# One TensorE-bound kernel: tanh rows by transposes in a second chunk, merged taps, a reordered tail, and a table of priority shifts

## The chip, the cores and the metric

The kernel runs on one core of one Trainium2 chip. TensorE (PE) multiplies matrices into PSUM; VectorE (DVE) and ScalarE (ACT) evict PSUM and do the elementwise work; GpSimd (POOL) does small copies and memsets; SyncE (SP) issues nearly all DMAs. The engines run beside each other, each through its own list in order, and wait for one another by semaphores. The metric is the device time of one execution in microseconds; the median of three runs is given, and one execution is profiled.

## The reference

The forward pass of a speech joint network and its gradients, all in bf16 with batch 2, 16000 time steps, width 256, 8 label positions:

```
h  = gelu(conv3(x, w1))[:, ::2]          # 3 taps, every second step kept
f  = gelu(conv3(h, w2))[:, ::2]          # 4000 steps remain
fe = f @ w_f ;  ge = g @ w_g
j  = tanh(fe[:, :, None, :] + ge[:, None, :, :])
out = j @ w_o                            # [2, 4000, 8, 256]
```

Returned are `out` and the gradients of x, w1, w2, g, w_f, w_g and w_o for a given `grad_out` of the shape of `out`.

## The kernel before

**Chunks.** The 2 × 4000 output steps are cut into 17 chunks (k = 0 to 16): one of 256 steps, fifteen of 512, one of 64. Chunk k goes through three stages. `stage_a` does both convolutions with gelu and its derivative, fe, and row-major copies for the weight gradients (FR, FER by transposes on TensorE, HRo and HRe by DMA transposes). `stage_j` does the joint network for four pairs of label positions: the tanh tile JT (feature-major, ACT, L643), its row-major twin JR, the product with w_o (OUT_SB), grad_out times w_o transposed (from GOT, a DMA transpose of GO), the tanh derivative 1 − JT² (JSQ, then NGZ and the sum ZS on DVE, ending as NGFE), and w_o's gradient GWO from JR and GO. `stage_de` does the backward pass: GF, GHe, GHo, the weight gradients (helper `wgrad`, sums ACC1, ACC2, ACCF by `acc_add`), and grad x (GX_SB). While chunk k is in `stage_j`, chunk k + 1 is in `stage_a` and chunk k − 1 in `stage_de`.

**JR in two ways.** For chunks in `TRANS` (only chunk 0 before) JR is made from JT by transposes on TensorE into a bf16 PSUM tile (psb) and a copy by ACT or DVE. For the others DVE adds FER and GEB (L667) and ACT takes a second tanh (L672); for these, `stage_a` also makes FER by eight transposes and one copy.

**The order of the work** is written by a planner, the class `Flow`. Each operation is recorded with its engine or engines, a cost in ns, what it reads and writes, the buffers it takes, and a priority: a due time in units of output steps (512 to a full chunk) set by `F.now` or `at`, plus a shift looked up in `SHIFT` by the stage's name and a part of it. `issue` is a list scheduler: with the costs it keeps a clock for each engine, and again and again takes the operation that can start first, by priority among equals. An operation with two engines (`evac`, and the square JSQ) goes to whichever can start it first. The result is one fixed list for each engine. Before the change `SHIFT` is empty.

The stages' names in that table: "a", "j" and "d" for `stage_a` of the next chunk, `stage_j`, and `stage_de` of the chunk before, followed by the step's number 0 to 3, "s" for the steps from 4 on, and "e" for the last ones; loads carry the step alone. Parts are "jt", "jr", "jsq", "gwo", "out" in `stage_j`, "late" for the gelu derivative, "dma", "xc", "go", "got" for transfers.

**Grad x.** For each block of rows and each pair of its four output offsets, twelve products of 256 columns by blocks of w1 transposed are formed, six to a PSUM tile; offset pairs read GHo and GHe.

**The end.** The last chunk's weight gradients are subtracted into staging tiles on DVE (L763) and stored by SP.

Of the kernel before, what the change touches and what calls it, by code (L numbers as in the profile page):

```python
# [30 lines left out]

class Op:
    __slots__ = ("eng", "cost", "fn", "deps", "soft", "succ", "left", "prio", "new", "bufs", "done", "work", "n",
                 "ready", "kind", "span")


class Flow:
# [27 lines left out]
        b.seq, s[0] = s[0], s[0] + 1  # L65
        return b

    def op(self, eng, cost, fn, r=(), w=(), new=(), at=None, work=0.0, after=(), kind=None, behind=(), sub=None):
        o = Op()
        o.eng = (eng,) if isinstance(eng, str) else tuple(eng)  # L70
        o.cost = cost if isinstance(cost, tuple) else (cost,) * len(o.eng)
        o.fn, o.new, o.work, o.n = fn, list(new), work, len(self.ops)
        o.prio = ((self.now if at is None else at) + self.shift.get((self.stage, sub), 0.0), o.n)
        o.succ, o.done, o.ready, o.kind, o.span = [], None, 0.0, kind, None
        deps, bufs = set(after), []
        for lst, wr in ((r, False), (w, True)):
            for x in lst:
                b, key = x if isinstance(x, tuple) else (x, None)
                for d, k, dw in b.log:
                    if (wr or dw) and (k is None or key is None or k == key):  # L80
                        deps.add(d)
                if b not in bufs:
                    bufs.append(b)
        for lst, wr in ((r, False), (w, True)):
            for x in lst:
                b, key = x if isinstance(x, tuple) else (x, None)
                if wr:
                    b.log = [e for e in b.log if not (key is None or e[1] == key)]
                b.log.append((o, key, wr))
        for b in o.new:  # L90
            b.born = o
        deps.discard(o)
        o.soft = ({b.born for b in bufs if b.born is not None} | set(behind)) - deps - {o}
        deps |= o.soft
        for b in o.new:
            if b not in bufs:
                bufs.append(b)
        o.deps, o.bufs = deps, bufs
        for b in bufs:
            b.users += 1  # L100
        o.left = len(deps)
        for d in deps:
            d.succ.append(o)
        self.ops.append(o)
        return o

    def issue(self):
# [10 lines left out]
        head = {c: 0 for c in queue}  # L118

        def put(o):  # L120
            o.ready = max((d.span[0] if d in o.soft else d.done for d in o.deps), default=0.0)
            for e in o.eng:
                avail[e].append(o)

# [83 lines left out]
def c_pe(ns):  # L208
    return sum(max(n / 2.4 + 2.5, 25.0) for n in ns)
# [11 lines left out]
def kernel(  # L221
# [28 lines left out]
    KT = 2  # L250
# [9 lines left out]
    sizes.append(NP - sum(sizes))  # L260
    assert sum(sizes) == NP

    SHIFT = {}
    TRANS = (0,)

    class Chunk:
        pass
# [70 lines left out]
    def fl(ap, A):  # L338
        return ap.rearrange("p (a c) -> p a c", a=A)
# [138 lines left out]
            r=rd, w=[(X, "m")], bytes_=(c.Pw - lo) * nr * 512, new=new, at=at, after=after)  # L478
        return X

    def rows(k, cls, name, SRC, lo, n, r, at=None, pe=0):
        R = buf(cls, [P, n if cls != "hro" else NB + 1, D], BF16, name)
        if pe:
            tr = psum(BF16)

            def trs(e):
                for a in range(n):
                    for kt in range(KT):
                        nc.tensor.transpose(out=tr[:pe, a * D + kt * P:a * D + (kt + 1) * P], in_=SRC[:, lo + a, kt, :pe],  # L489
                                            identity=ident[:])  # L490
            op("PE", c_pe([P] * (n * KT)), trs, r=(r or [SRC]) + [ident], w=[tr], new=[tr], at=at)
            evac(lambda: R[:pe, 0:n].rearrange("p a d -> p (a d)"), lambda: tr[:pe, 0:n * D], n * D, r=[tr], w=[R], new=[R], f=0.58)
            return R
        dma("SP", lambda: R[:, 0:n].rearrange("p a (k d) -> p (a k) d", d=P),
            lambda: SRC[:, lo:lo + n].rearrange("p a k c -> p (a k c)"), r=[SRC] if r is None else r, w=[R],
            bytes_=n * 65536, new=[R], transpose=True, at=at)
        return R

    def conv_gelu(c, taps, rd, h_buf, h_lo, g_buf, g_lo, news):
# [3 lines left out]
        for mt in range(KT):  # L503
            ps = psum()

            def mms(e, mt=mt, ps=ps):
                for k, (wt, rhs) in enumerate(taps):
                    mm(fl(ps[:, :W], A), wt(mt), rhs(), k == 0, k == len(taps) - 1)
            op("PE", c_pe([W] * len(taps)), mms, r=rd, w=[ps], new=[ps] + ([sq, s] + news if mt == 0 else []))
            op("ACT", c_act(W, True), lambda e, mt=mt, ps=ps: nc.scalar.activation(  # L510
                out=sq[:, 0:A, mt, :Pw], in_=fl(ps[:, :W], A), func=ACT.Square, scale=GELU_SQRT_K), r=[ps], w=[(sq, mt)])
            op("ACT", c_act(W, True), lambda e, mt=mt, ps=ps: nc.scalar.activation(  # L512
                out=h_buf[:, h_lo:h_lo + A, mt, :Pw], in_=fl(ps[:, :W], A), func=ACT.Gelu_apprx_tanh),
               r=[ps], w=[(h_buf, mt)])
            op("DVE", c_dve(W), lambda e, mt=mt, ps=ps: nc.vector.scalar_tensor_tensor(  # L515
                out=s[:, 0:A, mt, :Pw], in0=sq[:, 0:A, mt, :Pw], scalar=1.0, in1=fl(ps[:, :W], A),
                op0=ALU.add, op1=ALU.mult), r=[(sq, mt), ps], w=[(s, mt)])
# [19 lines left out]
    def stage_a(k, t0, dt):  # L537
# [51 lines left out]
            op("PE", c_pe([W] * KT), mms, r=[(FT, 0), (FT, 1), WF], w=[ps], new=[ps] + ([FE] if mt == 0 else []))  # L589
            evac(lambda mt=mt: FE[:, 0:A, mt, :Pw], lambda ps=ps: fl(ps[:, :W], A), W, r=[ps], w=[(FE, mt)])  # L590
        if k not in TRANS:
            S["FER"] = rows(k, "fer", "FER", FE, 0, A, [(FE, 0), (FE, 1)], pe=Pw)
        F.now = t0 + 0.5 * dt
        S["HRo"] = rows(k, "hro", "HRo", HTo, 0, A + 1, None)
        S["HRe"] = rows(k, "hre", "HRe", HTe, 0, A, None)
# [161 lines left out]
    def acc_add(ACC, key, acc_ap, ps, k, out):  # L757
        if k == NG - 1:
            t_ = buf({id(ACCF): "jr", id(ACC2): "jt", id(ACC1): "go"}[id(ACC)], [P, 2 * D], BF16, "stage")

            def flat():
                return t_[:]
            op("DVE", c_dve(512), lambda e: nc.vector.scalar_tensor_tensor(  # L763
                out=flat(), in0=acc_ap().rearrange("p k d -> p (k d)"), scalar=-1.0, in1=ps[:],
                op0=ALU.mult, op1=ALU.subtract), r=[(ACC, key), ps], w=[t_], new=[t_])
            dma("SP", lambda: out.rearrange("(dt p) n -> p dt n", p=P),
                lambda: flat().rearrange("p (k d) -> p k d", d=D), r=[t_], w=[], bytes_=131072)
        elif k == 0:
            evac(lambda: acc_ap().rearrange("p k d -> p (k d)"), lambda: ps[:], 512, r=[ps], w=[(ACC, key)])
        else:  # L770
            op("DVE", c_dve(512), lambda e: nc.vector.tensor_tensor(  # L771
                out=acc_ap().rearrange("p k d -> p (k d)"), in0=acc_ap().rearrange("p k d -> p (k d)"), in1=ps[:],
                op=ALU.add), r=[(ACC, key), ps], w=[(ACC, key)])

    def stage_de(k, t0, dt):
# [112 lines left out]
        if c.px is not None:  # L888
# [3 lines left out]
            op("POOL", 100.0, lambda e: nc.gpsimd.memset(GHz[:, :, c.px:c.px + 1], 0.0), w=[GHz])  # L892
            dma("SP", lambda: GHzR[:].rearrange("p (k d) -> p k d", d=P), lambda: GHz[:].rearrange("p k c -> p (k c)"),
                r=[GHz], w=[GHzR], bytes_=65536, transpose=True)
        rows4 = [[(GHo, 0, 0), (GHe, 0, 2)], [(GHo, 0, 1)], [(GHe, 1, 0), (GHo, 0, 2)], [(GHe, 1, 1)]]
        GX = None
        for bl, m in c.sblk:
            if bl % 2 == 0:
                GX = buf("gx", [P, 2, 4, D], BF16, "GX_SB")
            for cp in range(2):  # L900
                ps = psum()
                jobs = []
                for cj in range(2):
                    l = [(SRC, off, i, kt) for SRC, off, i in rows4[2 * cp + cj] for kt in range(KT)]
                    jobs += [(cj, n == 0, n == len(l) - 1) + a for n, a in enumerate(l)]

                def mms(e, jobs=jobs, ps=ps, bl=bl, m=m):
                    for cj, s_, e_, SRC, off, i, kt in jobs:
                        src = SRC[:, off + bl, kt, :m]
                        if GHz is not None and bl == 0 and off == 1 and i == 0:  # L910
                            src = GHz[:, kt, :m]
                        mm(ps[:m, cj * D:(cj + 1) * D], src, W1T[:, kt, i * D:(i + 1) * D], s_, e_)
                op("PE", c_pe([D] * len(jobs)), mms, r=[GHo, GHe, W1T] + ([GHz] if GHz is not None else []), w=[ps],
                   new=[ps] + ([GX] if cp == 0 and bl % 2 == 0 else []))
                evac(lambda m=m, cp=cp, GX=GX, bl=bl: GX[:m, bl % 2, 2 * cp:2 * cp + 2].rearrange("p c d -> p (c d)"),
                     lambda m=m, ps=ps: ps[:m, :], 512, r=[ps], w=[(GX, (bl % 2, cp))], scale=-1.0)
# [1 line left out]
            if bl % 2 == 1 or bl == A - 1:  # L918
# [13 lines left out]
                    put(0, Pw, 0, n)  # L932
                if c.ext and h == 0:
                    put(Pw, Pw + 1, 0, 3)
        for i in range(KK):
            def xl(da):
                return lambda a, m, d2: X[:m, 4 * a + da, d2 * P:(d2 + 1) * P]

            def he(a, m, i=i):
                return GHzR[:m, :] if GHzR is not None and i == 0 and a == 0 else GHeR[:m, a, :]  # L940
            wgrad(ACC1, i, lambda i=i: ACC1[:, i],
                  [(xl(i), rr(GHoR), c.sblk, [X, GHoR]),
                   (xl(i + 2), he, c.sblk, [X, GHeR] + ([GHzR] if GHzR is not None else []))], out_2[i])
            tick()

    def store(dst, src, r, scale=None):
        t_ = buf("gsq", [P, NB, KT, P], BF16, "g_sq")
# [180 lines left out]
```

## Time and profile before

| what | value |
|---|---|
| median of 3 runs | 798.06 us (797.32 to 798.76) |
| profiled execution | 797.41 us, its span 795.6 us |
| granted TensorE clock, mean | 0.996 |
| PE / weight loads busy | 774.8 / 559.2 us |
| DVE / ACT busy | 725.2 / 720.7 us |
| POOL busy | 67.5 us |

The span is from the first to the last instruction of the profiled execution. A PE matmul's end is modelled, so PE's busy time says when it had work, and its pace is read from the starts. Groups of instructions are named by line, engine, operation and tiles; nearly all matmuls stand under one helper's line (L336) and all copies out of PSUM under L345 or L347 (ACT) and L350 or L352 (DVE), so the tile's name tells them apart.

### The profile page before, as it was taken

The page shows a single profiled execution, that of the slowest core. Times are in us where ns is not written, and L with a number is a line of the kernel's source. Part 1 is how long each engine was busy: PE and PEld are TensorE (multiplying, and loading weights), DVE is VectorE, ACT ScalarE, POOL GpSimd, SP SyncE. Part 2 cuts the span into 40 slices and gives each one's busy share as a digit, 9 for nine tenths or more (in the row PEclk, how much of TensorE's full clock was granted, in tenths as well). Part 3 has the DMA queues.
Part 4 walks back from the last instruction along what each step waited for, and adds up shares of the span by engine and source line. Part 5 has one row for each costly group of instructions (what it writes and reads, how often), then busy time and mean ns, then how long its engine had stood idle before and what let it go on. Part 6 is the DMA issues. An engine that isn't in the chain of part 4 may idle for free.

```text
span 795.6 us, 16104 instructions
## 1 busy us (share of the span) xinstructions
PE 774.8 (97%) x5916; PEld 559.2 (70%) x5916; DVE 725.2 (91%) x1535; ACT 720.7 (91%) x1164; POOL 67.5 (8%) x227
## 2 busy tenths in 40 slices
PE   7989899999999999999999999999999999999996
PEld 6657578676776767768576685767868677687875
DVE  5899999998989989899998998989989999999964
ACT  6999999999898998989989899898999989899742
POOL 2020100101000010210100001010010100102010
PEclk9999999999999999999999999999999999999999
DMA  9999999999999999999999999999999999899994
GB/s 195 213 193 206 249 233 230 259 220 221 218 248 234 231 220 205 238 248 214 230 250 239 202 225 219 242 251 229 216 235 254 235 212 212 211 261 202 261 205 123
DMA packets 381811, 178.85 MB, mean 225 GB/s; under 512 B 307586, under 2 KB 375460, under 8 KB 379812
## 3 DMA queue, kind: packets, MB, share of 16 engines
q1 hardware_dynamic: 380788, 177.16, 99.7%
q8 instruction: 46, 0.75, 0.4%
q10 hardware_dynamic: 784, 0.39, 0.2%
q14 instruction: 33, 0.27, 0.1%
q0 software_dynamic: 160, 0.27, 0.1%
HBM read 51.42 MB, written 50.34 MB: 128 GB/s over the span
## 4 chain that ended last, share of the span: by engine, by line
PE 55%; ACT 24%; DVE 14%; issue 4%; DMA 3%; SPq 0%; DVEq 0%; ACTq 0%
PE ps L336 45%; PE GWO L336 8%; ACT JT L643 5%; ACT JR L672 4%; ACT JSQ L702 4%; ACT OUT_SB L345 3%; DVE g_s L515 3%; DVE NGZ L715 2%; ACT GX_SB L347 2%; ACT g_sq L510 1%; DVE ZS L732 1%; DMA GO<-in_grad_out_dram 1%; PE psb L489 1%; DMA out_dram<-OUT_SB 1%; DVE ACC L771 1%
## 5 line engine op out<-in xcount | busy, mean ns | idle before, releaser
L643 ACT ACTIVATE JT<-FE,GE 128x512 bf16<-128x512 bf16 (+4 forms) x288 | 190.7, 723 | 0.3 <-PE ps L336 0.3
L715 DVE SCALAR_TENSOR_TENSOR NGZ<-JSQ,ps 128x512 f32<-128x512 bf16 (+3 forms) x252 | 152.3, 613 | 1.6 <-PE ps L336 1.5
L336 PE MATMUL ps<-WO,JT 128*128 128x256 bf16 (+1 forms) x1008 | 150.0, 274 | 0.7 <-ACT JT L643 0.6
L336 PE MATMUL ps<-GOT,WOT 128*128 128x512 bf16 (+2 forms) x544 | 149.3, 363 | 0.4 <-DMA GOT<-GO 0.4
L672 ACT ACTIVATE JR<-JR 128x1024 bf16<-128x1024 bf16 (+1 forms) x124 | 136.2, 1101 | 12.8 <-DVE JR L667 12.8
L345 ACT CAST OUT_SB<-ps 128x512 bf16<-128x512 f32 (+1 forms) x215 | 132.7, 629 | 12.7 <-PE ps L336 12.5
L336 PEld LDWEIGHTS <-JT 128*128 128x128 bf16 (+1 forms) x1008 | 98.8, 98 | 57.9 <-issue 1.3
L702 ACT ACTIVATE JSQ<-JT 128x1024 bf16<-128x1024 bf16 (+2 forms) x123 | 128.7, 1046 | 10.0 <-DVE NGZ L715 7.7
L336 PE MATMUL GWO<-GO,JR 128*128 128x256 bf16 (+1 forms) x1008 | 131.4, 274 | 4.5 <-ACT JR L672 4.3
L732 DVE TENSOR_TENSOR ZS<-ZS,NGZ 128x1024 f32<-128x1024 f32 (+2 forms) x102 | 115.8, 1135 | 0.5
L336 PEld LDWEIGHTS <-JR 128*128 128x128 bf16 (+1 forms) x1008 | 98.0, 98 | 24.1 <-ACT JR L672 6.3
L336 PEld LDWEIGHTS <-W 128*128 128x128 bf16 x612 | 57.9, 98 | 59.7 <-issue 2.8
L515 DVE SCALAR_TENSOR_TENSOR g_s<-g_sq,ps 128x512 bf16<-128x512 bf16 (+2 forms) x102 | 65.1, 641 | 34.0 <-ACT HTo L512 32.7
L667 DVE TENSOR_TENSOR JR<-FER,GEB 128x1024 bf16<-128x1024 bf16 (+1 forms) x124 | 84.1, 684 | 3.1 <-PE GWO L336 2.3
L336 PE MATMUL ps<-XC,W 128*128 128x512 bf16 (+2 forms) x408 | 84.5, 362 | 1.7 <-DMA XC<-in_x_dram 1.7
L336 PEld LDWEIGHTS <-X 128*128 128x128 bf16 (+1 forms) x756 | 73.9, 98 | 9.0 <-DMA HRo<-HTo 0.2
L771 DVE TENSOR_TENSOR ACC<-ACC,ps 128x512 f32<-128x512 f32 x90 | 60.8, 684 | 20.1 <-PE ps L336 19.3
L336 PE MATMUL ps<-W1T,GHo 128*128 128x256 bf16 (+1 forms) x378 | 72.1, 273 | 0.0
L336 PE MATMUL ps<-W1T,GHe 128*128 128x256 bf16 (+1 forms) x376 | 71.8, 273 | 0.0
L510 ACT ACTIVATE g_sq<-ps 128x512 bf16<-128x512 f32 (+2 forms) x102 | 62.2, 610 | 8.6 <-PE ps L336 6.0
L336 PEld LDWEIGHTS <-WOT 128*128 128x128 bf16 x544 | 51.8, 98 | 22.9 <-DMA GOT<-GO 0.7
L347 ACT ACTIVATE GX_SB<-ps 128x512 bf16<-128x512 f32 (+1 forms) x98 | 59.2, 640 | 5.4 <-PE ps L336 4.9
(139 smaller groups left out, 1123.4 us busy)
## 6 DMA issues: line engine op xcount, KB each, us to landing
GO<-in_grad_out_dram SPq DMA_DIRECT2D x60, 512.0 KB, 5.6
out_dram<-OUT_SB SPq DMA_DIRECT2D x60, 512.0 KB, 6.1
X<-in_x_dram SPq DMA_DIRECT2D x15, 1088.0 KB, 7.4
out_dram<-GX_SB SPq DMA_DIRECT2D x30, 512.0 KB, 4.5
GO<-in_grad_out_dram SPq DMA_DIRECT2D x5, 256.0 KB, 5.3
GOT<-GO SPq DMA_TRANSPOSE x65, 4.7
out_dram<-OUT_SB SPq DMA_DIRECT2D x4, 256.0 KB, 3.5
XC<-in_x_dram SPq DMA_TRANSPOSE x62, 4.4
```

The costliest lines, as they stand in the source:

```text
L336: nc.tensor.matmul(ps_ap, lhsT=lhsT, rhs=rhs, start=start, stop=stop)
L345: nc.scalar.copy(out=dst(), in_=src())
L347: nc.scalar.activation(out=dst(), in_=src(), func=ACT.Copy, scale=scale)
L510: op("ACT", c_act(W, True), lambda e, mt=mt, ps=ps: nc.scalar.activation(out=sq[:, 0:A, mt, :Pw], in_=fl(ps[:, :W], A), func=ACT.Square, s ...
L515: op("DVE", c_dve(W), lambda e, mt=mt, ps=ps: nc.vector.scalar_tensor_tensor(out=s[:, 0:A, mt, :Pw], in0=sq[:, 0:A, mt, :Pw], scalar=1.0, ...
L643: nc.scalar.activation(out=fl(JT[:, j, mt, :W], A)[:, :, lo:hi], in_=FE[:, 0:A, mt, lo:hi], func=ACT.Tanh, bias=GE[:, b, mt, 2 * up + j:2 ...
L667: op("DVE", c_dve(n * 2 * D, 0.5), lambda e, lo=lo, n=n, m=m, JR=JR: nc.vector.tensor_tensor(out=JR[:m, 0:n], in0=S["FER"][:m, lo:lo + n]. ...
L672: op("ACT", c_act(n * 2 * D), lambda e, n=n, m=m, JR=JR: nc.scalar.activation(out=JR[:m, 0:n], in_=JR[:m, 0:n], func=ACT.Tanh), r=[JR], w= ...
L702: nc.scalar.activation(out=JSQ[:, :, :W], in_=JT[:, j, :, :W], func=ACT.Square)
L715: nc.vector.scalar_tensor_tensor(out=fl(zap(), A)[:, :, lo:hi], in0=fl(JSQ[:, d2, :W], A)[:, :, lo:hi], scalar=1.0, in1=fl(ps[:, :W], A)[: ...
L732: nc.vector.tensor_tensor(out=a, in0=a, in1=b, op=ALU.add)
L771: op("DVE", c_dve(512), lambda e: nc.vector.tensor_tensor(out=acc_ap().rearrange("p k d -> p (k d)"), in0=acc_ap().rearrange("p k d -> p ( ...
```

## The change

Six things, of which the last reaches everywhere:

- `TRANS` becomes `(0, 1)`: chunk 1 too gets JR by transposes and copies, and no FER.
- The planner takes a `lag`: FER's transposes count as ready 500 ns after fe's eviction, but for the first chunk.
- In the first chunk the square (g_sq) is due 8 units later than before, so that it goes behind gelu.
- In grad x the products that share a left operand and use adjacent blocks of w1 transposed are merged: two matmuls of 512 columns and two of 256 take the place of six of 256. The block at the border between the two batch entries, which has its own copy GHz, keeps one of its pairs apart.
- For the last chunk, two of the three w1 gradients are recorded ahead of grad x, and the last of them is stored by ACT's queue.
- `SHIFT` gets a table of priority shifts by stage and part.

In the built programs the total of PE's matmuls falls by 194: 252 fewer in grad x, 64 more transposes of JT, 8 fewer of FE, and two of the border block kept apart. The engine of 45 OUT_SB copies and 15 GX_SB copies changes from ACT to DVE. The other engines' counts follow from JR's way in chunk 1.

```diff
-    SHIFT = {}
-    TRANS = (0,)
+    SHIFT = {
+        ("1", "xc"): 32, ("2", "go"): -64, ("2", "got"): -272, ("a0", "late"): 256, ("a2", "dma"): 8,
+        ("a3", "late"): -32, ("ae", None): 64, ("ae", "late"): 64, ("as", "dma"): 320, ("as", "late"): 256,
+        ("d0", None): 32, ("d2", None): 16, ("j0", "jsq"): -32, ("j0", "out"): 8, ("j1", "jr"): 128,
+        ("j1", "jsq"): -256, ("j1", "out"): 64, ("j2", None): 48, ("j2", "dma"): 64, ("j2", "gwo"): -256,
+        ("j3", None): 128, ("j3", "dma"): -64, ("j3", "out"): -256, ("je", None): -32, ("je", "jt"): 8,
+        ("je", "out"): 64, ("js", None): -32, ("js", "gwo"): -248, ("js", "out"): 16, ("s", "go"): -16,
+        ("s", "got"): 64,
+    }
+    TRANS = (0, 1)
...
-            o.ready = max((d.span[0] if d in o.soft else d.done for d in o.deps), default=0.0)
+            o.ready = max((d.span[0] if d in o.soft else d.done for d in o.deps), default=0.0) + o.lag
...
-                out=sq[:, 0:A, mt, :Pw], in_=fl(ps[:, :W], A), func=ACT.Square, scale=GELU_SQRT_K), r=[ps], w=[(sq, mt)])
+                out=sq[:, 0:A, mt, :Pw], in_=fl(ps[:, :W], A), func=ACT.Square, scale=GELU_SQRT_K), r=[ps], w=[(sq, mt)],
+               at=F.now + 8.0 if c.first else None)
...
-            S["FER"] = rows(k, "fer", "FER", FE, 0, A, [(FE, 0), (FE, 1)], pe=Pw)
+            S["FER"] = rows(k, "fer", "FER", FE, 0, A, [(FE, 0), (FE, 1)], pe=Pw, lag=0.0 if c.first else 500.0)
...
-            dma("SP", lambda: out.rearrange("(dt p) n -> p dt n", p=P),
+            dma("ACT" if ACC is ACC1 and key == KK - 1 else "SP", lambda: out.rearrange("(dt p) n -> p dt n", p=P),
...
+        for i in range(2 if c.last else 0):
+            grad_w1(i)
...
-                def mms(e, jobs=jobs, ps=ps, bl=bl, m=m):
-                    for cj, s_, e_, SRC, off, i, kt in jobs:
-                        src = SRC[:, off + bl, kt, :m]
-                        if GHz is not None and bl == 0 and off == 1 and i == 0:
-                            src = GHz[:, kt, :m]
-                        mm(ps[:m, cj * D:(cj + 1) * D], src, W1T[:, kt, i * D:(i + 1) * D], s_, e_)
+                def mms(e, ps=ps, bl=bl, m=m, cp=cp, SA=SA, oa=oa, SB=SB, ob=ob):
+                    z = GHz is not None and bl == 0 and cp == 1
+                    for kt in range(KT):
+                        if z:
+                            mm(ps[:m, 0:D], GHz[:, kt, :m], W1T[:, kt, 0:D], kt == 0, False)
+                            mm(ps[:m, D:2 * D], SA[:, oa + bl, kt, :m], W1T[:, kt, D:2 * D], False, False)
+                        else:
+                            mm(ps[:m, 0:2 * D], SA[:, oa + bl, kt, :m], W1T[:, kt, 0:2 * D], kt == 0, False)
+                    for kt in range(KT):
+                        mm(ps[:m, 0:D], SB[:, ob + bl, kt, :m], W1T[:, kt, 2 * D:3 * D], False, kt == KT - 1)
...
-        for i in range(KK):
+        for i in range(2 if c.last else 0, KK):
+            grad_w1(i)
```

`grad_w1(i)` holds what the body of the old last loop held: one call of `wgrad` for tap i and one step of the due time.

More of the change, by code (lines that the diff above doesn't have):

```diff
@@ L33 @@
     __slots__ = ("eng", "cost", "fn", "deps", "soft", "succ", "left", "prio", "new", "bufs", "done", "work", "n",
-                 "ready", "kind", "span")
+                 "ready", "kind", "span", "lag")
 class Flow:
@@ L66, in buf, with op @@
         return b
-    def op(self, eng, cost, fn, r=(), w=(), new=(), at=None, work=0.0, after=(), kind=None, behind=(), sub=None):
+    def op(self, eng, cost, fn, r=(), w=(), new=(), at=None, work=0.0, after=(), kind=None, behind=(), sub=None, lag=0.0):
         o = Op()
@@ L73, in op @@
         o.prio = ((self.now if at is None else at) + self.shift.get((self.stage, sub), 0.0), o.n)
-        o.succ, o.done, o.ready, o.kind, o.span = [], None, 0.0, kind, None
+        o.succ, o.done, o.ready, o.kind, o.span, o.lag = [], None, 0.0, kind, None, lag
         deps, bufs = set(after), []
@@ L479, in load_x, with rows @@
         return X
-    def rows(k, cls, name, SRC, lo, n, r, at=None, pe=0):
+    def rows(k, cls, name, SRC, lo, n, r, at=None, pe=0, lag=0.0):
         R = buf(cls, [P, n if cls != "hro" else NB + 1, D], BF16, name)
@@ L490, in trs @@
                                             identity=ident[:])
-            op("PE", c_pe([P] * (n * KT)), trs, r=(r or [SRC]) + [ident], w=[tr], new=[tr], at=at)
+            op("PE", c_pe([P] * (n * KT)), trs, r=(r or [SRC]) + [ident], w=[tr], new=[tr], at=at, lag=lag)
             evac(lambda: R[:pe, 0:n].rearrange("p a d -> p (a d)"), lambda: tr[:pe, 0:n * D], n * D, r=[tr], w=[R], new=[R], f=0.58)
@@ L894, in stage_de, with grad_w1, xl, he @@
                 r=[GHz], w=[GHzR], bytes_=65536, transpose=True)
-        rows4 = [[(GHo, 0, 0), (GHe, 0, 2)], [(GHo, 0, 1)], [(GHe, 1, 0), (GHo, 0, 2)], [(GHe, 1, 1)]]
+        pairs4 = [(GHo, 0, GHe, 0), (GHe, 1, GHo, 0)]
+        def grad_w1(i):
+            def xl(da):
+                return lambda a, m, d2: X[:m, 4 * a + da, d2 * P:(d2 + 1) * P]
+            def he(a, m, i=i):
+                return GHzR[:m, :] if GHzR is not None and i == 0 and a == 0 else GHeR[:m, a, :]
+            wgrad(ACC1, i, lambda i=i: ACC1[:, i],
+                  [(xl(i), rr(GHoR), c.sblk, [X, GHoR]),
+                   (xl(i + 2), he, c.sblk, [X, GHeR] + ([GHzR] if GHzR is not None else []))], out_2[i])
+            tick()
+        for i in range(2 if c.last else 0):
+            grad_w1(i)
         GX = None
@@ L901, in stage_de @@
                 ps = psum()
[L902 to L905, printed above, removed]
-                def mms(e, jobs=jobs, ps=ps, bl=bl, m=m):
-                    for cj, s_, e_, SRC, off, i, kt in jobs:
-                        src = SRC[:, off + bl, kt, :m]
-                        if GHz is not None and bl == 0 and off == 1 and i == 0:
-                            src = GHz[:, kt, :m]
-                        mm(ps[:m, cj * D:(cj + 1) * D], src, W1T[:, kt, i * D:(i + 1) * D], s_, e_)
-                op("PE", c_pe([D] * len(jobs)), mms, r=[GHo, GHe, W1T] + ([GHz] if GHz is not None else []), w=[ps],
+                SA, oa, SB, ob = pairs4[cp]
+                def mms(e, ps=ps, bl=bl, m=m, cp=cp, SA=SA, oa=oa, SB=SB, ob=ob):
[8 more added lines that the diff above has]
+                        mm(ps[:m, 0:D], SB[:, ob + bl, kt, :m], W1T[:, kt, 2 * D:3 * D], False, kt == KT - 1)
+                op("PE", c_pe([2 * D] * 2 + [D] * 2), mms, r=[GHo, GHe, W1T] + ([GHz] if GHz is not None else []), w=[ps],
                    new=[ps] + ([GX] if cp == 0 and bl % 2 == 0 else []))
@@ L934, in stage_de @@
                     put(Pw, Pw + 1, 0, 3)
-        for i in range(KK):
[L936 to L944, printed above, removed]
+        for i in range(2 if c.last else 0, KK):
+            grad_w1(i)
     def store(dst, src, r, scale=None):
```

## The prediction

> **What bounds the kernel now.** I read the page first (busy shares and slices), then the busy times by stretch, the waits by engine, and the timeline at places where TensorE (PE) waits.
>
> ```profile
> span 795.6 us, 16104 instructions
> PE 774.8 (97%) x5916; PEld 559.2 (70%) x5916; DVE 725.2 (91%) x1535; ACT 720.7 (91%) x1164; POOL 67.5 (8%) x227
> PE   7989899999999999999999999999999999999996
> ...
> 20.00:40.00 20.00, 19.55 (x150) 13.12 (x149) 17.65 (x45) 19.63 (x36) 1.90 (x7) 1.00 1.12 213
> 40.00:60.00 20.00, 17.82 (x108) 10.84 (x107) 18.44 (x47) 19.08 (x30) 4.55 (x11) 0.91 1.09 192
> 60.00:80.00 20.00, 19.02 (x153) 14.29 (x152) 19.93 (x42) 19.74 (x33) 0.53 (x2) 1.00 0.96 211
> 80.00:100.00 20.00, 17.74 (x115) 10.40 (x113) 19.77 (x39) 20.00 (x33) 2.81 (x7) 1.00 1.04 243
> ...
> 200.00:250.00 50.00, 50.00 (x376) 35.91 (x375) 46.30 (x94) 47.40 (x74) 2.88 (x12) 1.00 1.04 228
> 250.00:300.00 50.00, 48.98 (x366) 35.03 (x365) 45.39 (x89) 47.22 (x74) 3.53 (x14) 1.00 1.00 226
> ```
>
> In the stretches the columns are length, busy time of PE, weight loads, VectorE (DVE), ScalarE (ACT), POOL, then granted clock, DMA share, GB/s. From 100 us on PE is full while DVE and ACT have 3 to 4 us spare in 50. Between 20 and 100 us it is the other way round: ACT is full (78.45 of 80), DVE nearly, and PE idles 80 − 74.13 = 5.9 us. So the kernel is PE-bound, but for the first two chunks, the waits below, and the ends.
>
> ```profile
> PE GWO L336 <- ACT JR L672: 4.3, 3, 1.7
> PE psb L489 <- ACT FE L345: 3.2, 9, 0.8
> PE ps L336 <- DVE NGFE L729: 0.8, 1, 0.8
> PEld L489 <- ACT FE L345: 5.4, 12, 0.9
> DVE g_s L515 <- ACT HTo L512: 32.7, 29, 7.1
> DVE ACC L771 <- PE ps L336: 19.3, 23, 2.0
> ```
>
> (total us, times, longest.) PE's waits have three places: for JR's tanh in the first chunks, for fe's eviction before its transposes in most chunks, and once for NGFE at the end.
>
> ```profile
> 307.22 0.60 PE L336 MATMUL ps<-GOT,WOT 128*128 128x512 bf16 x2
> 307.66 0.60 PE L336 MATMUL ps<-WO,JT 128*128 128x256 bf16 x4
> 308.09 0.61 PE L489 MATMUL psb<-ident,FT 128*128 128x128 bf16 x8
> 309.07 0.23 PE L489 MATMUL psb<-ident,FE 128*128 128x128 bf16 x1 [0.37 <-ACT FE L345]
> 309.56 0.56 PE L489 MATMUL psb<-ident,FE 128*128 128x128 bf16 x7 [0.26 <-ACT FE L345]
> 309.96 0.38 PE L336 MATMUL ps<-W1T,GHo 128*128 128x256 bf16 x2
> 310.18 0.38 PE L336 MATMUL ps<-W1T,GHe 128*128 128x256 bf16 x2
> ```
>
> Starts give the pace: two matmuls of 512 columns take 0.44 us (0.22 each), four of 256 take 0.43 (0.11 each), and eight transposes 0.61 less the last one's 0.23 of duration, over 7: 56 ns. A full chunk has 88 matmuls of 512, 256 of 256 and 16 transposes; with the unrounded 0.2155 and 0.1092 us that is 19.0 + 28.0 + 0.9 = 47.8 us of PE. Waits of about 0.5 us a chunk come on top (fe's 5.4 us below over 15 chunks, and small ones).
>
> **Second chunk's tanh by TensorE.** The changed program has in chunk 1 eight transposes for each of 8 halves, and 8 fewer for its FER: 64 − 8 = 56 × 56 ns = 3.1 us more of PE. It loses 8 JR tanhs on ACT, 8 JR additions on DVE and one FER copy; it gains 8 JR copies, of which its order gives 7 to ACT and 1 to DVE.
>
> ```profile
> 410.30 0.96 ACT JR L672
> 402.64 1.20 DVE ACC L771 x2
> L345 ACT COPY JR<-psb 128x1024 bf16<-128x1024 bf16 x3 | 3.1, 1037 | 0.0
> L672 ACT ACTIVATE JR<-JR 128x1024 bf16<-128x1024 bf16 x120 | 133.7, 1117 | 12.8 <-DVE JR L667 12.8
> ```
>
> The first two rows are of the chain of waits: a JR tanh holds ACT for 0.95, a DVE instruction over 512 columns 0.60. A JR copy is 0.08 shorter than the tanh: 0.9. ACT: −8 × 0.95 + 7 × 0.9 = −1.3 us. DVE: −8 × 0.60 − 0.6 + 0.6 = −4.8. Evictions can go to either engine, so shared it is −3.05 on each. The table also moves the "late" gelu derivatives of chunk 1 by 256 (half a chunk): 3 ACT tanhs (2.9 us) and 6.6 us of DVE (by the same pace) leave the crowded stretch for one where PE bounds, up to 4.7 more per engine. What PE can give back is its idle 5.9 plus the stretch at half clock:
>
> ```profile
> 44.00:46.00 2.00, 1.12 (x7) 0.85 (x8) 2.00 (x6) 2.00 (x3) 0.15 (x1) 0.78 1.26 207
> 46.00:47.00 1.00, 1.00 (x6) 0.72 (x5) 1.00 (x6) 0.87 (x2) 1.00 (x4) 0.50 1.28 238
> 47.00:48.00 1.00, 1.00 (x5) 0.46 (x3) 1.00 (x5) 0.51 (x2) 0.54 (x1) 0.50 1.28 216
> 48.00:49.00 1.00, 1.00 (x8) 0.73 (x7) 0.38 (x2) 1.00 (x3) 0.00 (x0) 0.74 0.64 118
> ```
>
> 0.44 + 0.5 + 0.5 + 0.26 = 1.7 us of clock lost, so 7.6 us in all, less the 3.1 us of added transposes: at most −4.5. At least −1.3, if ACT alone bounds and nothing is postponed. I take −3.8, near the upper end, because removal and postponement together (7.7) exceed what PE can give. Late next is PE itself. The Trainium skill, "TensorE: Matmul & The Clock Gate", Part 1, says that the clock halves after an idle window of some 3.4 us and comes back after a busy one of that length. The trace agrees (3.4 us at 0.50, behind the waits for JR); by that rule the 1.7 us goes only if chunk 0's waits shrink, and without it this term would be −2.1.
>
> **Later fe transposes.** A lag of 500 ns in the planner puts more work between fe's matmuls and its transposes: in the order, PE work between them is 1.37 us in 8 of 16 chunks before, and about 2.0 after. The waits are 3.2 us (PE's row) to 5.4 (weight loads'). Taken: −4.5; bounds 0 (evictions come later by as much) and −5.4. The cover is other matmuls of the chunk; who waits for FER is the next chunk's JR addition, far off.
>
> **Merged taps.** 126 groups of six 256-column matmuls become two of 512 and two of 256: 6 × 0.1092 = 0.655 against 2 × 0.2155 + 2 × 0.1092 = 0.649. Columns are the same, so 0 to −0.8; taken −0.3. The skill's same page ("Wait — 56ns, not 53.3ns?") has N/2.4 GHz + 2.5 ns for each matmul; with 252 fewer that would be −0.6.
>
> **Start.** In chunk 0 gelu now goes ahead of square:
>
> ```profile
> 7.42 0.38 ACT L510 ACTIVATE g_sq<-ps 128x256 bf16<-128x256 f32 x1 [4.72 <-PE ps L336]
> 7.70 0.38 ACT L512 ACTIVATE HTo<-ps 128x256 bf16<-128x256 f32 x1
> ```
>
> Each conv of the startup chain is ready 0.28 earlier, of three: 0 to −0.8, taken −0.6. What is late then is DVE's gelu derivative, which has slack.
>
> **Tail.** In the order, chunk 15's 48 weight-gradient matmuls now stand ahead of NGFE's, which covers the 0.8. The last result:
>
> ```profile
> 777.34 0.38 PE L336 MATMUL ps<-NGFE,WFT 128*128 128x64 bf16 x4 [0.82 <-DVE NGFE L729]
> 789.40 1.28 DVE L763 SCALAR_TENSOR_TENSOR stage<-ACC,ps 128x512 bf16<-128x512 f32 x2
> 790.56 1.73 SPq L362 DMA_DIRECT2D out_dram<-stage  x3
> ```
>
> The data is done at 790.7; SP issues its third store at about 791.9. On ACT's queue it goes at once (nothing is behind it there), and SP's second ends 0.7 earlier. So 0.8 + 0.7 = −1.5; but the small chunk's chain NGFE, GF, GHe, GHo now has less work beside it, which may cost up to +1.0 net. Taken −1.2.
>
> **The table.** Moving priorities changes no work, only places and engine: by the order DVE takes 45 OUT_SB and 15 GX_SB copies and 5 squares more than before. 65 × 0.60 = 39 us, with the other exchanges (fewer JR additions and FER and GEB copies, four FE and some small ones more) +34 net; ACT loses some 30. DVE: 725.2 + 34 = 759 of about 785, 97% (98% in full chunks: 46.9 of 47.8 us). Hidden while PE is longer: 0. SP's queue has one store fewer; its transposes of grad_out now go two in a row at the end of each chunk, behind HRe's:
>
> ```profile
> 357.25 2.87 SPq L360 DMA_TRANSPOSE GOT<-GO  x1
> 368.90 0.59 PE L336 MATMUL ps<-GOT,WOT 128*128 128x512 bf16 x2
> DMA to landing us min/median/max: 4.3/4.6/7.8
> ```
>
> That one was issued 11.7 us before its use and lands in 4.3 to 7.8; a transpose put behind another of 2.9 still comes in time. Taken 0. POOL's halos are not moved past anything that PE was seen to wait for.
>
> Sum: −0.6 − 3.8 − 4.5 − 0.3 − 1.2 = −10.4 us, on the profiled execution's 797.41 us (span 795.6): 787.0. That run lies 0.65 under the median 798.06, so the median becomes 787.7.
>
> **Rivals.**
> 1. *DVE becomes the bound (slower).* DVE runs its list in order; in the rows above it waited 32.7 + 19.3 = 52 us for ACT and PE, 3.2 a chunk. With 46.9 us of work per chunk it can afford 0.9. If x stays, a chunk takes 46.9 + x against 48.3 before; with the other terms (−5.9) it turns slower from x = 1.9. At x = 2.6: 13 × 1.2 − 5.9 = +9.7, 808. For it: the shift of 34 us. Against: many of these waits are of an engine with nothing else to do.
> 2. *Waits move.* JR's copies come on ACT, which is full, and fe's evictions slip with their transposes: −1.3 − 1.5 − 0.3 − 0.6 − 0.5 = −4.2, 793.9. For it: fe's eviction was late because ACT or DVE held something longer, and DVE is now fuller.
> 3. *All of it goes:* every term at its end, −4.5 − 5.4 − 0.8 − 0.8 − 1.5 = −13.0, and what the matmuls' modelled ends hide (a wait shows some 0.2 us shorter than it is; about 20 waits, 4 us): 781.
> 4. *Loads come late:* with 5 us less margin on GOT, 0.7 a chunk for 13 chunks is +9, 797.
>
> **How the numbers follow.** Chances: forecast 0.52 (783 to 791), rival 1 0.12, rival 2 0.18, rival 3 0.14, rival 4 0.04. What a measurement can tell from no change is 0.2%, 1.6 us. Faster: 0.52 + 0.14 + most of 0.18 + a little: 0.83; same 0.06; slower 0.11. The range leaves out rival 1 and the far end of rival 3: 780 to 798.
>
> **What would show it.** PE's waits for JR and FE gone from the list; stretch 20 to 100 with PE over 78 of 80 and no clock of 0.50; no 0.8 wait for NGFE; the last store on ACT's queue; DVE busy near 759, ACT near 690. It is wrong if PE in the middle shows idle time released by DVE (rival 1), or by DMA (rival 4).

## The result, and the profile after

The changed kernel takes 794.16 us (median; 793.42 to 794.34) against 797.79 us of the kernel before in the same comparison: a ratio of 0.994, interval 0.9923 to 0.9958 (the two medians alone give 0.995). It is faster, as forecast, but by 3.6 us where 10.4 were forecast.

The page of the changed kernel, its first lines, and then busy times by stretch (columns as before):

```profile
span 792.5 us, 15639 instructions
PE 775.1 (98%) x5692; PEld 534.8 (67%) x5722; DVE 752.6 (95%) x1591; ACT 692.3 (87%) x1099; POOL 76.4 (10%) x227
...
20.00:40.00 20.00, 19.65 (x152) 13.20 (x150) 18.18 (x49) 19.00 (x37) 2.36 (x8) 1.00 1.12 203
40.00:60.00 20.00, 18.39 (x148) 13.13 (x148) 19.93 (x47) 19.53 (x31) 2.58 (x10) 1.00 1.02 185
60.00:80.00 20.00, 19.98 (x163) 13.99 (x162) 19.68 (x42) 19.57 (x33) 0.66 (x2) 1.00 1.04 238
80.00:100.00 20.00, 19.95 (x147) 13.93 (x147) 20.00 (x42) 19.60 (x29) 1.18 (x5) 1.00 1.07 235
...
200.00:250.00 50.00, 49.35 (x351) 33.38 (x352) 49.80 (x101) 41.02 (x61) 4.19 (x14) 1.00 1.06 235
250.00:300.00 50.00, 49.58 (x362) 34.41 (x362) 49.76 (x97) 45.09 (x66) 4.95 (x12) 1.00 1.03 226
```

The first 100 us are much better: PE is busy 78.0 of 80 us where it was 74.1, and the clock of 0.91 is 1.00. From 200 to 300 us, DVE has taken PE's place: 49.8 of 50 us, where it had 46.3 and 45.4 before, and ACT has 5 to 9 us spare. How full PE is cannot be read from its busy time here, since some of its matmuls are missing from this trace; the sum below corrects for them.

The waits of the changed kernel (total us, times, longest):

```profile
PE GWO L345 <- ACT JR L682: 1.6, 6, 0.3
PEld L345 <- ACT JR L682: 12.1, 32, 0.8
ACT JR L682 <- DVE JR L677: 16.2, 19, 2.3
DVE ACC L781 <- PE ps L345: 11.6, 8, 5.2
DVE g_s L525 <- ACT HTo L522: 6.1, 10, 1.2
```

The waits for fe's eviction have nearly gone: of the weight loads' 5.7 us, 1.0 is left. In their place weight loads wait 32 times for JR's tanh on ACT. Before there were six such waits, none of them between 100 and 750 us:

```profile
PEld L336 <- ACT JR L672: 6.7, 6, 2.2
```

That tanh waits 19 times for JR's addition on DVE. It did so 14 times before, too (12.8 us), but then PE did not wait behind it in the middle. One such place in the timeline of the changed kernel:

```profile
227.78 0.68 DVE L359 CAST OUT_SB<-ps 128x512 bf16<-128x512 f32 x1
228.38 0.68 DVE L677 TENSOR_TENSOR JR<-FER,GEB 128x1024 bf16<-128x1024 bf16 x1
...
229.09 1.06 ACT L682 ACTIVATE JR<-JR 128x1024 bf16<-128x1024 bf16 x1 [0.74 <-DVE JR L677]
...
230.20 0.77 PEld L345 LDWEIGHTS <-JR 128*128 128x128 bf16 x8 [0.81 <-ACT JR L682]
230.21 1.05 PE L345 MATMUL GWO<-GO,JR 128*128 128x256 bf16 x8 [0.32 <-ACT JR L682]
```

DVE evicts an OUT_SB ahead of JR's addition, ACT idles 0.74 us until that addition is done, and GWO's products wait for ACT.

**PE's time as a sum.** The tables below use one measure. The distance between the starts of neighbouring matmuls, less the pace of the first (0.2155, 0.1092 and 0.056 us for 512, 256 and 128 columns, as in the prediction), is waiting, and it is summed over a stretch. The traces of kernels with merged taps lack 30 to 37 of 5722 matmuls; these are put in from the order of the built program. All in us of the profiled execution:

| kernel | PE work | waits 0 to 20 | 20 to 100 | 100 to 750 | from 750 | after the last matmul | span |
|---|---|---|---|---|---|---|---|
| before | 762.1 | 5.9 | 9.7 | 7.4 | 3.3 | 6.0 | 795.6 |
| changed | 764.6 | 5.6 | 3.2 | 8.6 | 2.3 | 6.9 | 792.5 |

Add 1.1 us ahead of the first matmul. The change pays 2.5 us of PE work, gains 6.5 in the first chunks, 0.3 at the start and 1.0 in the tail, and loses 1.2 in the middle and 0.9 after the last matmul: 3.2 us in all. The middle should have given 4.5 us and took 1.2: that is most of the 6.8 us that are missing.

By the same measure, what PE waited ahead of in the middle has changed. Ahead of fe's transposes it was 6.0 us before and is 0.6 now; ahead of GWO's products, which need JR, it was nothing before and is 4.3 now.

### The profile page after: what moved, and what is told of

Its sections match the earlier page's. It is cut to its first block, busy times and chain, and to the rows that moved or that the text cites. A ratio compares the mean times of both kernels' runs of the same rounds, so it can differ in the third digit from the quotient of the medians.

```text
span 792.5 us, 15639 instructions
## 1 busy us (share of the span) xinstructions
PE 775.1 (98%) x5692; PEld 534.8 (67%) x5722; DVE 752.6 (95%) x1591; ACT 692.3 (87%) x1099; POOL 76.4 (10%) x227
## 5 line engine op out<-in xcount | busy, mean ns | idle before, releaser
L653 ACT ACTIVATE JT<-FE,GE 128x512 bf16<-128x512 bf16 (+4 forms) x288 | 180.2, 678 | 0.1
L345 PE MATMUL ps<-WO,JT 128*128 128x256 bf16 (+1 forms) x1008 | 146.6, 273 | 0.1
L712 ACT ACTIVATE JSQ<-JT 128x1024 bf16<-128x1024 bf16 (+2 forms) x120 | 119.5, 996 | 23.4 <-DVE NGZ L725 16.2
L682 ACT ACTIVATE JR<-JR 128x1024 bf16<-128x1024 bf16 (+1 forms) x116 | 120.8, 1056 | 16.6 <-DVE JR L677 16.2
L354 ACT CAST OUT_SB<-ps 128x512 bf16<-128x512 f32 (+1 forms) x170 | 97.5, 592 | 14.0 <-PE ps L345 13.5
L677 DVE TENSOR_TENSOR JR<-FER,GEB 128x1024 bf16<-128x1024 bf16 (+1 forms) x116 | 77.7, 679 | 1.0 <-PE GWO L345 1.0
L519 ACT ACTIVATE g_sq<-ps 128x512 bf16<-128x512 f32 (+2 forms) x102 | 58.1, 572 | 10.4 <-DVE G1o L544 5.1
L534 ACT ACTIVATE g_s<-g_s 128x1024 bf16<-128x1024 bf16 (+2 forms) x51 | 51.0, 1004 | 10.1 <-DVE g_s L525 10.0
L345 PE MATMUL ps<-W1T,GHe 128*128 128x256 bf16 (+2 forms) x247 | 58.5, 324 | 1.3
L345 PE MATMUL ps<-GHoR,X 128*128 128x256 bf16 (+1 forms) x378 | 57.7, 273 | 0.0
```

The lines of the kernel that those rows point to most:

```text
L345: nc.tensor.matmul(ps_ap, lhsT=lhsT, rhs=rhs, start=start, stop=stop)
L354: nc.scalar.copy(out=dst(), in_=src())
L534: op("ACT", c_act(N), lambda e: nc.scalar.activation(out=v(s), in_=v(s), func=ACT.Tanh, scale=k_), r=[s], w=[s], at=late, sub="late")
L653: nc.scalar.activation(out=fl(JT[:, j, mt, :W], A)[:, :, lo:hi], in_=FE[:, 0:A, mt, lo:hi], func=ACT.Tanh, bias=GE[:, b, mt, 2 * up + j:2 ...
L677: op("DVE", c_dve(n * 2 * D, 0.5), lambda e, lo=lo, n=n, m=m, JR=JR: nc.vector.tensor_tensor(out=JR[:m, 0:n], in0=S["FER"][:m, lo:lo + n]. ...
L682: op("ACT", c_act(n * 2 * D), lambda e, n=n, m=m, JR=JR: nc.scalar.activation(out=JR[:m, 0:n], in_=JR[:m, 0:n], func=ACT.Tanh), r=[JR], w= ...
```

## Experiments

Theory A: the table of shifts hands so many evictions to DVE that it is full in every chunk, and PE waits for what DVE delivers late. Theory B: the middle's waits have another cause (the places of JR and GWO in the lists, or a table that works only as one piece).

### The table taken out, and the table alone

```diff
-    SHIFT = { ... }
+    SHIFT = {}
```

> The changed kernel with an empty table of shifts; everything else of the change stays. Theory A (the table hands 34 us of copies to DVE, which then is full in every chunk, and PE's waits for fe come back as waits for what DVE delivers): without the table DVE falls back to about 720 us busy, the waits for fe stay away because of the lag, and the time is 788 to 790. Theory B (the table is what brings the gain, and the waits of the middle have another cause): 796 to 799.

> The kernel before with the table and nothing else. Theory A: the table's load on DVE without the relief of the second chunk's transposes, DVE busy 755 to 765, time 799 to 803. Theory B: the table brings most of the gain by itself, 794 to 796.

Without the table: 793.99 us, ratio to before 0.9945 (0.9927 to 0.9963). With the table alone on the kernel before: 802.27, ratio 1.0035 (1.0013 to 1.0058).

| kernel | 20 to 100 | 100 to 750 | from 750 | after the last | DVE busy | ACT busy |
|---|---|---|---|---|---|---|
| changed | 3.2 | 8.6 | 2.3 | 6.9 | 752.6 | 692.3 |
| changed, no table | 6.2 | 4.0 | 4.4 | 5.2 | 716.6 | 727.5 |
| before, table alone | 11.5 | 9.1 | 3.6 | 5.7 | 758.6 | 694.4 |

Both outcomes go against a simple reading. The first expectation of theory A failed in its number (794.0, not 788 to 790), though its mechanism is there: without the table DVE drops by 36 us and the middle's waits from 8.6 to 4.0. What was missed is that the table earns elsewhere: 3.0 us in the first chunks, and 2.1 in the tail, of which 1.7 are lost again behind the last matmul. Of the 3.0, about 1.7 are the clock: without the table it was granted at 0.60 and 0.55 from 44 to 48 us of this one profiled execution, with it at 1.00. As a whole the table is worth nothing in time (794.16 with it, 793.99 without). The second run bears theory A out: alone the table makes the kernel slower, with DVE at 758.6.

### DVE's load changed, the lists kept

One run shortens a DVE instruction and one adds another, while the planner still reckons with the old cost, so that every engine's list is otherwise the same. (Cuts of the code; the lighter kernel leaves out half of each sum, so some of its gradients are incomplete.)

```diff
-                            nc.vector.tensor_tensor(out=a, in0=a, in1=b, op=ALU.add)
+                            h = W // 2
+                            nc.vector.tensor_tensor(out=a[:, :, :h], in0=a[:, :, :h], in1=b[:, :, :h], op=ALU.add)
```

> The changed kernel with the same lists on every engine, but the running sum ZS on DVE adds only half of its columns (the planner's costs are unchanged; the gradients that go through NGFE are left incomplete). DVE has 0.53 us less in each of 6 sums, 3.2 us less per full chunk. Theory A: PE's waits between 100 and 750 us, 8 to 9 us in all, fall to 3 or less, time 788 to 790. Theory B: nothing waits for DVE's length, 793 to 794.5.

```diff
                             nc.vector.tensor_tensor(out=a, in0=a, in1=b, op=ALU.add)
+                            if W == CW:
+                                z = ZS[:, 0, 0:400]
+                                nc.vector.tensor_tensor(out=z, in0=z, in1=z, op=ALU.max)
```

> The kernel before, with one more DVE instruction (0.48 us, a maximum of ZS with itself over 400 columns, which changes nothing) behind each of the 6 sums of a full chunk: 2.9 us more of DVE per chunk, about what the table adds, in lists that are otherwise those of before. Theory A: DVE at 97 to 98%, 4 to 8 us slower, 802 to 806. Theory B: within 1 us of before, 797 to 799.

The lighter DVE gives 787.77 us, ratio 0.9865 (0.985 to 0.9879). PE's waits in the middle fall from 8.6 to 3.1. Busy times from 100 to 750 us, of the changed kernel and then of the lighter one:

```profile
100.00:750.00 650.00, 645.60 (x4645) 442.14 (x4671) 640.38 (x1298) 585.00 (x906) 60.95 (x172) 1.00 1.02 231
```

```profile
100.00:750.00 650.00, 647.80 (x4692) 448.01 (x4717) 607.70 (x1302) 587.21 (x913) 58.38 (x174) 1.00 1.03 233
```

DVE goes from 98.5% to 93.5% busy, ACT stays. Over the whole span DVE has 40 us less (752.6 to 712.2), 2.7 a chunk where 3.2 were expected. With the same lists 6.4 us are back, and the waits ahead of GWO's products fall from 4.3 to 0.6 us. So, in these lists, the length of DVE's work is what held 5.5 of the middle's 8.6 us.

The heavier DVE on the kernel before takes 834.6 us, ratio 1.0453 (1.0435 to 1.0472). That was expected 4 to 8 us slower and is 36. A line of its page:

```profile
PE 785.5 (94%) x5916; PEld 560.2 (67%) x5916; DVE 772.6 (93%) x1625; ACT 723.7 (87%) x1164; POOL 72.8 (9%) x227
```

The added instruction, then waits of DVE and of PE:

```profile
L735 DVE TENSOR_TENSOR ZS<-ZS x90: 574/576/968, 59.0 to 792.4; 128x400 f32<-128x400 f32 x90
DVE g_s L515 <- ACT HTo L512: 37.5, 31, 7.4
DVE ACC L774 <- PE ps L336: 7.0, 7, 1.9
PE psb L489 <- ACT FE L345: 12.4, 15, 1.7
```

90 instructions of 0.576 us (0.48 expected) are at most 52 us; DVE's busy time rose by 47, and the time by 36. DVE's waits for PE ahead of the ACC sums shrank (7.0 us, before 19.3), but those for ACT's HTo did not (37.5, before 32.7): only a part of its idle time was room for more work. The stretch from 100 to 750 us, before and with the heavier DVE:

```profile
100.00:750.00 650.00, 646.50 (x4914) 468.18 (x4913) 609.79 (x1237) 612.99 (x965) 48.95 (x170) 1.00 1.02 230
100.00:750.00 650.00, 624.00 (x4643) 444.18 (x4641) 619.63 (x1237) 584.97 (x904) 49.97 (x160) 1.00 0.97 219
```

PE's waits in it rise from 7.4 to some 37 us, half of them ahead of fe's transposes. With 47.8 us of PE work to a full chunk, a chunk then takes about 48.3 us before and 50.6 here, and DVE's work in it is about 45.4 and 48.3: its idle time went from 3.0 us a chunk to 2.4 only. Without a gap DVE would need 48.3 us, as long as a chunk took before; the 2.3 us more are idle time that stayed. In the changed kernel, whose lists were written anew for the load, DVE's work is about 47.7 of 48.4 us, with 0.7 of idle. So DVE can be filled to 98.5% if the lists are planned for it, and nearly the same load in lists that were not costs 2 us a chunk more. What the load costs depends on the lists.

### Which part of the table

Seven of its entries act on the steps from 4 on ("as", "js", "s"). The diffs of this part show the entries alone, without the rest of their lines.

```diff
-        ("as", "dma"): 320, ("as", "late"): 256, ("js", None): -32, ("js", "gwo"): -248, ("js", "out"): 16,
-        ("s", "go"): -16, ("s", "got"): 64,
```

> The changed kernel without those seven entries of the table that act on the steps from 4 on; the entries for the first steps and the last ones stay. Its order gives DVE 41 OUT_SB and 27 GX_SB copies instead of 82 and 43. Theory A (the steady entries fill DVE and cost 4 to 5 us in the middle, the first ones bring 3 us, the last ones 2): PE's waits 3.5 between 20 and 100 us and 4 between 100 and 750, time 788 to 791. Theory B (the table is one piece and its effects do not add): 793 to 796.

788.61 us, ratio 0.9885 (0.9868 to 0.9901): theory A. Of this kernel, page and stretch:

```profile
span 787.7 us, 15706 instructions
PE 773.4 (98%) x5690; PEld 538.6 (68%) x5722; DVE 719.5 (91%) x1526; ACT 723.8 (92%) x1164; POOL 87.8 (11%) x227
...
100.00:750.00 650.00, 647.64 (x4685) 448.68 (x4714) 611.34 (x1242) 621.45 (x983) 71.40 (x173) 1.00 1.03 233
```

PE's waits are 3.4 us in the first chunks, 2.8 in the middle, 3.0 in the tail: the gain of the first entries stays and the middle's waits go, with DVE and ACT even again. It beats both kernels.

Two runs take only some of the steady entries out:

```diff
-("as", "late"): 256,
```

> The changed kernel without the one table entry that postpones the gelu derivatives in the steady steps by half a chunk. Its order gives DVE 94 OUT_SB and 25 GX_SB copies, as much as the change (82 and 43). If the load on DVE is what costs: no faster than the change, 793 to 796, DVE busy 745 to 760. Rival (the postponed derivatives themselves block DVE's list): 788 to 790.

```diff
-("js", None): -32, ("js", "gwo"): -248, ("js", "out"): 16,
```

> The changed kernel without the three table entries that act on the joint stage of the steady steps. Its order gives DVE 61 OUT_SB and 39 GX_SB copies, 25 fewer than the change (15 us less of DVE). If the load on DVE is what costs, it lies between the change and the table without its steady entries: 790 to 792, PE's waits in the middle 5 to 7 us. Rival (the places of GWO's products and of JR, not DVE's load): 788 to 789.

793.70 us (ratio 0.9933, 0.9914 to 0.9953) and 793.89 (0.9942, 0.9927 to 0.9957). Waits in the middle are 7.9 and 7.2, DVE's busy time 742.6 and 738.7. The first has the time that theory A expected; DVE's busy time lies just under the 745 to 760. The second was expected at 790 to 792 and is no faster than the change. A part of that is not the middle's doing: its tail waits 4.2 us, the changed kernel's 2.3, of which 0.9 come back behind the last matmul. In the middle the waits for JR have nearly gone; in their place stand waits for GF (2.8 us ahead of GF's products, 0.3 in the changed kernel), and weight loads that wait with no releaser shown ("issue", over the span 18.3 us, in the changed kernel 8.8):

```profile
PE ps L345 <- DVE GF L808: 1.7, 4, 0.7
PEld L345 <- ACT JR L682: 0.8, 3, 0.4
PEld L345 <- issue: 18.3, 47, 1.2
```

So neither part alone is the culprit, and what PE waits for depends on the part; what stays is DVE's load. Among the kernels with the lag, the middle's waits go with DVE's busy share there: 2.8 to 4.0 us at 93.0 to 94.1% (the lighter DVE, no steady entries, no table), 7.2 at 96.2%, 7.9 at 96.9%, 8.6 at 98.5%. The kernel without the lag (below) lies between, 6.3 us at 95.3%. Only the lighter DVE has this with unchanged lists; in the others the lists differ too.

### The lag

On the kernel before:

```diff
-            S["FER"] = rows(k, "fer", "FER", FE, 0, A, [(FE, 0), (FE, 1)], pe=Pw)
+            S["FER"] = rows(k, "fer", "FER", FE, 0, A, [(FE, 0), (FE, 1)], pe=Pw, lag=0.0 if c.first else 500.0)
```

> The kernel before with the lag of 500 ns ahead of FER's transposes, nothing else. If the prediction's term holds (the lag by itself takes the waits for fe away, 4.5 us): 793 to 795, PE's waits for FE under 1.5 us. Rival (evictions come later by as much, or the wait turns up at another matmul): 796.5 to 798.5.

On the kernel without steady entries:

```diff
-lag=0.0 if c.first else 500.0
+lag=0.0
```

> The table without its steady entries, and without the lag ahead of FER's transposes. If the lag is worth nothing by itself also here: 788 to 790, PE's waits in the middle 3 to 4 us. If it is what keeps the waits for fe away beside the other edits: those come back, 792 to 795.

Alone on the kernel before: 799.06 us, ratio 1.0009 (0.9992 to 1.0025), no gain. Its waits for fe:

```profile
PE psb L489 <- ACT FE L345: 1.6, 7, 0.3
PEld L489 <- ACT FE L345: 4.8, 12, 0.5
```

PE's row is halved, the weight loads' is not (5.4 before), and the middle's waits stay at 7.3 us. By the starts, the waits ahead of fe's transposes fall from 6.0 to 4.5 us, and those ahead of GF's and grad x's products rise by as much (1.0 to 2.6): a part of the wait turned up at other matmuls. In its order the PE work between fe's matmuls and FER's transposes rose from 1.37 us to about 2.0 where it had been short; but in the trace fe's second eviction ends 2.18 us behind the last fe matmul (mean over 13 chunks), where it was 1.85. So the lists were written anew with the eviction 0.33 us later; the work put between rose by 0.6 us or so in half of the chunks, which is about as much in the mean.

Taken out of the kernel without steady entries, it costs 4.5 us, or 3.7 by the two ratios to before: 793.15, ratio 0.9932 (0.9917 to 0.9947). The waits for fe are back:

```profile
PEld L497 <- ACT FE L353: 1.9, 6, 0.4
PEld L497 <- DVE FE L358: 1.1, 2, 0.7
```

They are 2.7 of 6.3 us in the middle by PE's measure. Not only the lag differs, though: this order also has 64 OUT_SB copies on DVE, where the one with the lag has 41. The two cannot be told apart here, since one edit rewrites every list.

### The single parts

```diff
-    TRANS = (0,)
+    TRANS = (0, 1)
```

> The kernel before with JR of the second chunk by transposes, nothing else. If the prediction's term holds without the table's postponement: PE's waits between 20 and 100 us fall from 9.7 to 4 or 5 against 3.1 us of added transposes, 795.5 to 797. Rival (copies on a full ACT put the waits back): 798 or more.

796.50 us, ratio 0.9982 (0.9968 to 0.9996); as expected. The waits from 20 to 100 us fall from 9.7 to 4.9, against 3.1 us of transposes.

```diff
-            dma("ACT" if ACC is ACC1 and key == KK - 1 else "SP",
+            dma("SP",
```

> The changed kernel with its last store on SP's queue again. By the prediction's term it is 0.7 us slower: 794.6 to 795.2. Rival (the span ends with SP's queue of stores either way, each about 0.53 us): 0 to 0.5 us slower, too little to tell.

793.96 us, against 794.16: no slower, as the rival had it. The end of the changed kernel's timeline:

```profile
784.35 2.03 SPq L371 DMA_DIRECT2D out_dram<-stage  x4
784.80 1.88 DVE L773 SCALAR_TENSOR_TENSOR stage<-ACC,ps 128x512 bf16<-128x512 f32 x3 [0.45 <-PE ps L345]
786.47 0.96 SPq L371 DMA_DIRECT2D out_dram<-GX_SB  x2
786.71 0.39 ACTq L371 DMA_DIRECT2D out_dram<-stage  x1
787.52 0.91 SPq L371 DMA_DIRECT2D out_dram<-stage  x2
```

ACT's store goes out as soon as its data is there (786.7), but SP has eight stores in a row from 784.35 on, some 0.5 us each, and issues the last at 788.0, 1.3 us after the last result. Moving one store to ACT's queue left SP's queue to end last.

> The table without its steady entries, with grad x's products apart again, twelve of 256 columns to a block (the same places in every list). By the rows of before the merge is worth 0 to 0.8 us: 788.4 to 789.5. Rival (the longer matmuls or their order cost something): faster than 788.

```diff
-                            mm(ps[:m, 0:2 * D], SA[:, oa + bl, kt, :m], W1T[:, kt, 0:2 * D], kt == 0, False)
+                        mm(ps[:m, 0:D], (GHz[:, kt, :m] if z else SA[:, oa + bl, kt, :m]), W1T[:, kt, 0:D], kt == 0, False)
...
+                    for kt in range(KT):
+                        mm(ps[:m, D:2 * D], SA[:, oa + bl, kt, :m], W1T[:, kt, D:2 * D], kt == 0, kt == KT - 1)
```

788.23 us, ratio 0.9869 (0.9853 to 0.9886), beside 788.61 (ratio 0.9885) with merged taps. It lies just under the expected range and just above the rival's; the two kernels cannot be told apart, and the merge shows no gain.

## Why the prediction was wrong

The direction and the mechanism of the first chunks held; the size did not, because of one step above all.

- **Second chunk's tanh and the postponement: right.** −3.8 was forecast; waits fell by 6.5 against 3.1 of transposes, −3.4. The parts show in the runs: transposes alone 9.7 to 4.9, and 3.2 with everything, 3.4 without the steady entries. The clock of 0.50 behind JR's waits is gone:

```profile
44.00:46.00 2.00, 1.53 (x17) 1.39 (x17) 2.00 (x6) 2.00 (x4) 0.00 (x0) 1.00 0.80 171
46.00:48.00 2.00, 2.00 (x28) 1.85 (x26) 2.00 (x6) 2.00 (x4) 0.84 (x2) 1.00 0.90 158
```

  The Trainium skill ("TensorE: Matmul & The Clock Gate", Part 1) has the half clock follow an idle window of some 3.4 us. The traces agree only in part. Before, the longest waits ahead of it were 0.7 and 1.8 us, and PE was busy 0.83 of the 3 us from 42 to 45. In the changed kernel the longest wait is 1.0 us, and no half clock follows. But with the transposes alone the longest waits there are 1.1, 0.7 and 1.4 us and the clock stays at 1.00, while without the table they are the same and the clock falls to 0.60 and 0.55. So what decides is not shown, and that the 1.7 us of clock came back may be the chance of one execution; without it the 3.4 would be 1.7.
- **The table, "Hidden while PE is longer: 0": this step failed.** It was priced by DVE's total, 98% of a chunk, and what was left of the chunk was taken for room enough. The total was right (752.6 us busy, forecast 759; ACT 692.3, forecast 690); the room was not there. The steady entries cost 5.8 us in the middle (2.8 against 8.6), 5.6 in the time (788.61 against 794.16), and with 40 us less of DVE in the same lists 6.4 us came back. That is rival 1, with a smaller price than I gave it: DVE kept 0 to 0.6 us of idle per 50 in 11 of 13 stretches, not the 2.6 a chunk that I priced. Such a price did show where work was added to lists that were not planned for it: the heavier DVE kept about 2.4 us of idle a chunk. The gain of the table's other entries, part of which the second chunk's term had priced, makes up for the loss: as a whole the table came out at nothing.
- **Later fe transposes, −4.5: wrong by itself, unsettled in company.** Its lower bound ("evictions come later by as much") is what the lag alone shows. Beside the other edits the waits for fe did go; without the table the middle's waits are 4.0 us, 3.4 less than before. In the changed kernel the time went to JR's waits.
- **Merged taps, −0.3:** not to be told from nothing. The Trainium skill ("TensorE: Matmul & The Clock Gate", "Wait — 56ns, not 53.3ns?") has some 2.5 ns for each matmul, by which 252 fewer would be an estimated 0.6 us. The paces here agree (2 × 0.1092 − 0.2155 us is 2.9 ns), but no run shows the time.
- **Start, −0.6:** waits ahead of 20 us fell by 0.3, and no run tests the reorder alone. They lie between about 5.5 and 7.2 us in the other profiled executions, with the reorder and without, so the 0.3 cannot be told from nothing.
- **Tail, −1.2:** PE's wait for NGFE is gone and the tail's waits fell by 1.0, but the time after the last matmul rose by 0.9. The term for the store (−0.7) was wrong: the end waits for SP's queue, not for one store.
- **GOT and the queue of loads, 0: right.** No wait for GOT shows in the changed kernel's list.

That the forecast of 787.7 lies beside the kernels in which DVE is at 94% in the middle (787.77, 788.61 and 788.23) is partly chance, since the terms of the tail, the start and the lag were off. That rival 2's 793.9 lies beside the measured 794.2 is chance too: it had the second chunk's tanh at −1.3, where the profiles show −3.4, and no loss by the steady entries.

## What to carry to other kernels

Do not take an engine's idle share for room: with a fixed order on each engine, idle time sits where the list waits, and work put elsewhere can add to the time. Here 33 us more of DVE, planned for, cost 5.6 us, and 47 us more in lists that were not planned for it cost 36; neither was free, and the price hung on the lists. A run with the same lists and a lighter instruction shows how much of the time hangs on the load. When a table of many moves is tuned as a whole, split it by the stage that it acts on and read each stage's waits: here it gained 3 us at the start (about half of that the clock), 2 in the tail, most of it lost again behind the last matmul, and lost 5 in the middle.

## What the runs showed that I had not expected

A DVE instruction of 0.576 us added six times a chunk to a kernel with DVE at 91% raised DVE's busy time by 47 us and the time by 36. And the traces of kernels with 512-column taps lack 30 to 37 of 5722 matmul records (5692 are in the page above, with 5722 weight loads), while those with taps apart lack none (5972 of 5972), so that busy time and count of PE are a little low in the changed kernel's page.
